# The experts' side work in another order: first weights of the next slot split a quarter sooner, the last conversion step inside the last quarter

## The chip, the core and the metric

The kernel runs on one core of one Trainium2 chip. The metric is device time in microseconds (us) of one execution; the time before is 1410.79 us, the median of three runs (1409.42 to 1414.0). The profiled execution is one more run of the same program, with a time of its own.

## The reference

Three layers follow each other. An attention without a product of queries and keys (the softmax of k over the tokens times v gives a 64 x 64 matrix for each head) makes 4608 tokens of 512 numbers. A mixture of eight experts sends every token to the expert with the largest gate logit:

```python
for e in range(E):
    mask = e_idx == e
    h = np.maximum(x[mask] @ w1[e], 0.0)
    out[mask] = gate_w[mask, None] * (h @ w2[e])
```

with w1[e] of 512 x 1024 and w2[e] of 1024 x 512. A dense layer `g = max(0.01 h, h)`, `h = x @ w_in`, `out = g @ w_out` (hidden width 2048) ends it; its weights arrive as 64-bit floats. All results are fp32.

## The kernel before, in words

**Products.** TensorE multiplies in a rounded 32-bit form. To keep fp32 accuracy, each operand is split into a high part (a cast on ScalarE, line 481) and a low part (source minus high part, a subtraction on VectorE, line 482), and each product is three matmuls: high by high, high by low, low by high. `split` is these two instructions.

**Slots.** The experts' tokens are worked off in slots of at most 512 tokens of one expert. Nine slots (0 to 8) always run; more run as the counts want, under a branch read from a register. In this input ten ran, the tenth (slot 9) in the half form with 256 rows.

A slot has two passes. The first, `pass1(f)` for f = 0 to 7, makes 128 hidden units each: 12 matmuls into a PSUM bank `hp`, then `hh` = relu (ScalarE, line 574) and `hl` = low part (VectorE, line 575). There are three `hp` banks, so the bank of f = 0 is wanted again by f = 3, and it is free once its `hl` is made. The second, `pass2(t)` for t = 0 to 3 (here called the four quarters), makes 128 output columns each: 24 matmuls into a bank `yp`, a copy `y` (ScalarE, line 589), and a store that ScalarE issues (line 590). After 12 of a quarter's 24 matmuls the function `mid` is called, and what it records stands on every engine in front of that quarter's copy.

**Side work.** While a slot is multiplied, the other engines do four things:
- `wsplit(s, which, c)` splits a quarter of a weight matrix: w2 of this slot in the first pass, w1 of the next slot (`w1h`, `w1l`) in the second. The source is a ring of six staging tiles `st`; each split lets SyncE issue the load of a later piece.
- `xload` at the slot's start turns token numbers into integers (`idi`, line 551) and gathers the next slot's rows into `xg`; `xgate` scales them; `xprep(k)` transposes them on TensorE (line 564, into `tp`, two PSUM banks) and splits them into `xh`, `xl`. `xprep(0)` and `xprep(1)` stand in the middle of quarter 1, `xprep(2)` and `xprep(3)` in the middle of quarter 2.
- `step()` runs one step of the conversion of the dense layer's weights from 64-bit floats: four steps make one conversion, and a slot has eight steps, two conversions. Step one also issues the two stores of the conversion before (`rh`, `rl`) and the loads for the next (`w`). Steps one to three are two VectorE instructions each. Step four is the heaviest: four sums `r` (line 631), a cast `rh` on ScalarE, and the subtraction `rl` on VectorE. It falls on f = 7 and on quarter 3.
- In slot 8 the step is a load of a weight of the dense layer, and `mid` of its quarter 3 also splits two operands of it.

**What sets the order.** Each engine runs its instructions in the order in which the Python code records them, and the framework adds the semaphores. No scheduler changes it here: where a call stands in `slot` is its place on each engine.

Of the kernel before, what the change touches and what calls it, by code (L numbers as in the profile page):

```python
# [25 lines left out]
NSLOT = 16  # L26
# [453 lines left out]
def split(nc, hi, lo, src):  # L480
    nc.scalar.copy(out=hi, in_=src)  # L481
    nc.vector.tensor_tensor(out=lo, in0=src, in1=hi.bitcast(F32), op=ALU.subtract)  # L482


def experts(ctx, tc, cst, a, region, xd, dense, did, wops, pre):
# [24 lines left out]
    def reg(s, f, mx):  # L510
        return nc.values_load(ti[0:1, 3 * s + f:3 * s + f + 1], engines=[SP] + [ACT] * (f == 2), min_val=0, max_val=mx)
# [17 lines left out]
    def loads_to(n):  # L529
        while nload[0] < min(n, len(items)):  # L530
            wload(*items[nload[0]])
            nload[0] += 1

    def wsplit(s, which, c):
        n = 8 * s + 4 * (which - 1) + c
        loads_to(n + 1)
        t = stage.pop((s, which, c))
        if which == 1:
            split(nc, w1h[:, :, 256 * c:256 * c + 256], w1l[:, :, 256 * c:256 * c + 256], t.rearrange("p (k f) -> p k f", k=4))
        else:  # L540
            split(nc, w2h[:, 2 * c:2 * c + 2], w2l[:, 2 * c:2 * c + 2], t.rearrange("p (k f) -> p k f", k=2))
        loads_to(n + 1 + AHEAD)

    def idload(s):
        if s < NSLOT:
            nc.sync.dma_start(out=idts[s % 3].rearrange("p t c -> p (t c)"),
                              in_=region[bass.ds(reg(s, 1, NE * NT), SLOT), :].rearrange("(p t) c -> p (t c)", t=4))

    def xload(s):
        idt, idi = idts[s % 3], idis[s % 2]  # L550
        nc.vector.tensor_copy(out=idi, in_=idt[:, :, 0])
        for t in range(4):
            nc.gpsimd.indirect_dma_start(out=xg[:, t], out_offset=None, in_=xd,  # L553
                                         in_offset=bass.IndirectOffsetOnAxis(ap=idi[:, t:t + 1], axis=0),
                                         bounds_check=NT - 1, oob_is_err=False)

    def xgate(s):
        for t in range(4):
            nc.scalar.activation(out=xg[:, t], in_=xg[:, t], func=AF.Copy, scale=idts[s % 3][:, t, 1:2])

    def xprep(k):
        tp = ps2.tile([128, 4, 128], F32, tag="tp", name="tp")
        for t in range(4):
            nc.tensor.transpose(out=tp[:, t], in_=xg[:, t, 128 * k:128 * k + 128], identity=ident)
        split(nc, *(x[:, k].rearrange("d (p t) -> d t p", t=4) for x in (xh, xl)), tp)

    def pass1(f, rows):
        hp = ps.tile([128, SLOT], F32, tag="h", name="hp")
        n = 0
        for k in range(4):  # L570
            for w, x in ((w1h, xh), (w1h, xl), (w1l, xh)):
                nc.tensor.matmul(hp[:, rows], lhsT=w[:, k, 128 * f:128 * f + 128], rhs=x[:, k, rows], start=(n == 0), stop=(n == 11))  # L572
                n += 1
        nc.scalar.activation(out=hh[:, f, rows], in_=hp[:, rows], func=AF.Relu)
        nc.vector.scalar_tensor_tensor(out=hl[:, f, rows], in0=hp[:, rows], scalar=0.0, in1=hh[:, f, rows].bitcast(F32),  # L575
                                       op0=ALU.max, op1=ALU.subtract)

    def pass2(d, o, mid, rows):
        yp = ps.tile([128, SLOT], F32, tag="y", name="yp")
        n = 0  # L580
        for f in range(8):
            for w, h in ((w2h, hh), (w2l, hh), (w2h, hl)):
                nc.tensor.matmul(yp[:, rows], lhsT=w[:, f, 128 * d:128 * d + 128], rhs=h[:, f, rows], start=(n == 0), stop=(n == 23))  # L583
                n += 1
            if f == 3:
                mid()
        y = ys[cnt[1] % 2]
        cnt[1] += 1
        nc.scalar.copy(out=y[:, rows], in_=yp[:, rows])
        nc.scalar.dma_start(out=dense[128 * d:128 * d + 128, bass.ds(o, rows.stop)], in_=y[:, rows])  # L590
# [65 lines left out]
    def slot(s, step=lambda: None, mid2=lambda t: None, rows=slice(0, SLOT)):  # L656
        if s + 1 < NSLOT:
            xload(s + 1)
        for f in range(8):
            pass1(f, rows)  # L660
            if f % 2 == 0:
                wsplit(s, 2, f // 2)
            else:
                step()
        if s + 1 < NSLOT:
            xgate(s + 1)
        o = reg(s, 2, NT)
        nc.sync.dma_start(out=did[bass.ds(o, SLOT)].rearrange("(p t) c -> p (t c)", t=4),
                          in_=idts[s % 3].rearrange("p t c -> p (t c)"))
        idload(s + 2)  # L670
        for t in range(4):
            def mid():
                if s + 1 < NSLOT and t in (1, 2):
                    xprep(2 * t - 2)
                    xprep(2 * t - 1)
                mid2(t)
            pass2(t, o, mid, rows)
            if s + 1 < NSLOT:
                wsplit(s + 1, 1, t)
            step()  # L680

    idload(0)
    loads_to(2)
# [9 lines left out]
    with ExitStack() as cctx:  # L693
        conv = conversions(cctx.enter_context(tc.tile_pool(name="cv", bufs=1, side="right", reuse_waits="tile")))
        next(conv)
        for s in range(NSTATIC - 1):
            slot(s, step=lambda: next(conv, None))
        for _ in conv:
            pass
    load, prep = pre()  # L700
    slot(NSTATIC - 1, step=lambda: next(load, None), mid2=lambda t: prep() if t == 3 else None)
    nb = nc.values_load(ti[0:1, 3 * NSLOT:3 * NSLOT + 1], min_val=0, max_val=NSLOT)
    ns = nc.values_load(ti[0:1, 3 * NSLOT + 1:3 * NSLOT + 2], min_val=NSTATIC, max_val=NSLOT)

    def more(s):
        if s == NSLOT:
            return
        with tc.If(ns > s):  # L708
            before = dict(stage), list(cnt), nload[0]
            regs.clear()  # L710
            with tc.If(nb > s) as big:
                slot(s)
            stage.clear()
            stage.update(before[0])
            cnt[:], nload[0] = before[1:]
            regs.clear()
            with big.Else():
                slot(s, rows=slice(0, SLOT // 2))
            regs.clear()
            more(s + 1)  # L720
# [393 lines left out]
```

## Time and profile before

| | |
|---|---|
| median of three runs | 1410.79 us |
| the profiled execution's own time | 1407.18 us |
| its span, first to last instruction | 1405.4 us |
| busy share TensorE / VectorE / ScalarE / GpSimd | 93% / 73% / 42% / 23% |
| mean granted TensorE clock | 0.974 |
| first matmul of slot 0, first matmul after slot 9 | 200.6 us, 657.45 us |

The experts are the stretch from 200.6 to about 657 us. To read them: the timeline of one engine gives each instruction's start and length, and in brackets how long the engine stood idle before it and what released it. A TensorE matmul is shown as longer than the distance to the next one, since matmuls overlap; the distance from start to start is what counts.

### The profile page before, as it was taken

The numbers are of one execution on the slowest core, as the hardware profiler recorded it, in microseconds if no ns is written. First come the engines' busy times: TensorE is split into PE (matmuls) and PEld (weight loads), VectorE is DVE, ScalarE is ACT, GpSimd is POOL, SyncE is SP. The second block draws the span as 40 slices with busy tenths as digits, with TensorE's granted clock in tenths as the row PEclk, the third lists the DMA queues.
The fourth block names the chain that finished last, engine by engine and source line by source line (L and its number), as shares of the span: only waits on it lengthen the run. The fifth ranks groups of instructions, "written<-read, shape, count | busy, mean of one in ns | idle before, by whom it ended". The sixth has DMA issues, their size and how long they took to land.

```text
span 1405.4 us, 23487 instructions
## 1 busy us (share of the span) xinstructions
PE 1306.8 (93%) x9179; PEld 1219.4 (87%) x9179; DVE 1029.1 (73%) x1392; ACT 585.5 (42%) x914; POOL 322.0 (23%) x279
## 2 busy tenths in 40 slices
PE   5989449999999999998999999999989999999998
PEld 5989337778777877788999999999989999999998
DVE  4788836776777677746777777787777777877785
ACT  3656235455545554555232333323233333333332
POOL 2225820110111011100333433434311111111111
PEclk9999769999999999998999999999999999999999
DMA  9773258787977797687933333233695443444330
GB/s 374 294 284 117 69 173 283 239 256 240 299 241 261 235 297 238 217 279 234 375 136 135 126 135 130 92 150 135 262 414 179 124 133 122 149 123 134 121 120 31
DMA packets 146969, 279.56 MB, mean 199 GB/s; under 512 B 18208, under 2 KB 70432, under 8 KB 145952
## 3 DMA queue, kind: packets, MB, share of 16 engines
q1 hardware_dynamic: 122064, 208.46, 44.0%
q10 hardware_dynamic: 17232, 48.48, 8.8%
q0 software_dynamic: 7552, 21.02, 4.2%
q8 instruction: 75, 1.23, 0.4%
q14 instruction: 46, 0.38, 0.1%
HBM read 181.59 MB, written 96.32 MB: 198 GB/s over the span
## 4 chain that ended last, share of the span: by engine, by line
issue 26%; DVE 8%; PE 8%; POOL 6%; DMA 3%; ACT 1%; POOLq 0%; SPq 0%; DVEq 0%; ACTq 0%
PE hp L801 8%; POOL out L982 3%; POOL s L841 2%; DMA wi<-wid 2%; DMA hd<-ht 2%; DVE ht L814 1%; DVE ht L847 1%; DVE ht L850 1%; DVE s L838 1%; DVE x L482 1%; DVE ht L834 1%; DVE s L836 1%; POOL s L842 1%; DVE xl L482 0%; ACT ht L843 0%
## 5 line engine op out<-in xcount | busy, mean ns | idle before, releaser
L801 PE MATMUL hp<-xh,wi 128*128 128x256 f32 x1152 | 212.9, 281 | 4.4 <-DVE ht L850 2.3
L960 PE MATMUL yp<-wi,x 128*128 128x256 f32 x1152 | 191.2, 283 | 0.3 <-DVE x L482 0.3
L801 PEld LDWEIGHTS hp<-xh,wi 128*128 128x128 f32 x1152 | 179.4, 188 | 7.0 <-DVE ht L850 3.5
L960 PE MATMUL yp<-wi,wi 128*128 128x256 f32 x1200 | 178.2, 283 | 0.3 <-DVE wi L482 0.3
L801 PE MATMUL hp<-x,wi 128*128 128x256 f32 x1296 | 164.2, 286 | 8.0 <-DVEq L708 6.5
L801 PEld LDWEIGHTS hp<-x,wi 128*128 128x128 f32 x1296 | 160.7, 194 | 8.3 <-ACTq L708 6.6
L960 PEld LDWEIGHTS yp<-wi,wi 128*128 128x128 f32 x1200 | 163.5, 192 | 0.5 <-DVE wi L482 0.5
L960 PEld LDWEIGHTS yp<-wi,x 128*128 128x128 f32 x1152 | 161.5, 192 | 0.6 <-DVE x L482 0.6
L801 PE MATMUL hp<-xl,wi 128*128 128x256 f32 x576 | 160.7, 279 | 0.0
L553 POOL DMA_INDIRECT xg<-xd,idi x44 | 55.4, 1259 | 399.4 <-DVE hl L575 349.6
L572 PE MATMUL hp<-xh,w1h 128*128 128x512 f32 (+1 forms) x320 | 122.9, 384 | 12.7 <-DVE hl L575 11.6
L583 PE MATMUL yp<-hh,w2h 128*128 128x512 f32 (+1 forms) x320 | 122.9, 384 | 0.0
L572 PE MATMUL hp<-xl,w1h 128*128 128x512 f32 (+1 forms) x320 | 121.5, 380 | 0.0
L583 PE MATMUL yp<-hl,w2h 128*128 128x512 f32 (+1 forms) x320 | 121.5, 380 | 0.0
L572 PE MATMUL hp<-xh,w1l 128*128 128x512 f32 (+1 forms) x320 | 121.4, 379 | 0.0
L583 PE MATMUL yp<-hh,w2l 128*128 128x512 f32 (+1 forms) x320 | 121.4, 379 | 0.0
L982 POOL DMA_INDIRECT out<-yo,idx x36 | 47.3, 1315 | 315.4 <-DVE idx L976 294.3
L482 DVE TENSOR_TENSOR w1l<-st,w1h 128x1024 fp32r<-128x1024 f32 x44 | 53.7, 1225 | 75.2 <-ACT w1h L481 75.1
L801 PEld LDWEIGHTS hp<-xl,wi 128*128 128x128 f32 x576 | 108.0, 187 | 0.0
L814 DVE SCALAR_TENSOR_TENSOR ht<-ht 128x1024 f32<-128x1024 f32 x72 | 104.9, 1457 | 2.5
L841 POOL TENSOR_TENSOR s<-s,s 128x512 f32<-128x512 f32 x36 | 48.6, 1351 | 207.9 <-DVE s L838 155.6
L843 ACT ACTIVATE ht<-s 128x512 f32<-128x512 f32 x36 | 22.8, 633 | 149.5 <-POOL s L842 145.1
(202 smaller groups left out, 2581.4 us busy)
## 6 DMA issues: line engine op xcount, KB each, us to landing
st<-in_w SPq DMA_DIRECT2D x89, 512.0 KB, 6.0
hd<-ht ACTq DMA_DIRECT2D x72, 512.0 KB, 3.0
xt<-hd SPq DMA_DIRECT2D x18, 1024.0 KB, 5.5
hr<-hd SPq DMA_DIRECT2D x18, 1024.0 KB, 5.5
wi<-wid SPq DMA_DIRECT2D x28, 512.0 KB, 10.7
wi<-wod SPq DMA_DIRECT2D x6, 2048.0 KB, 12.7
v<-in_v SPq DMA_DIRECT2D x16, 650.0 KB, 9.9
k<-in_k SPq DMA_DIRECT2D x16, 576.0 KB, 8.8
```

The lines of the kernel that those rows point to most:

```text
L482: nc.vector.tensor_tensor(out=lo, in0=src, in1=hi.bitcast(F32), op=ALU.subtract)
L553: nc.gpsimd.indirect_dma_start(out=xg[:, t], out_offset=None, in_=xd, in_offset=bass.IndirectOffsetOnAxis(ap=idi[:, t:t + 1], axis=0), bou ...
L572: nc.tensor.matmul(hp[:, rows], lhsT=w[:, k, 128 * f:128 * f + 128], rhs=x[:, k, rows], start=(n == 0), stop=(n == 11))
L583: nc.tensor.matmul(yp[:, rows], lhsT=w[:, f, 128 * d:128 * d + 128], rhs=h[:, f, rows], start=(n == 0), stop=(n == 23))
L801: self.nc.tensor.matmul(bank[:, g], lhsT=w[:, h, k, 128 * g:128 * g + 128], rhs=x[:, k], start=(n == 0), stop=(n == 5))
L814: V.scalar_tensor_tensor(out=c, in0=c, scalar=0.01, in1=c, op0=ALU.mult, op1=ALU.max)
L834: V.tensor_tensor(out=h[:, 0, 0], in0=bank, in1=s[1], op=ALU.add)
L836: V.tensor_tensor(out=s[6], in0=bank, in1=s[1], op=ALU.add)
L841: G.tensor_tensor(out=s[6], in0=s[6], in1=s[5], op=ALU.add)
L843: nc.scalar.activation(out=h[:, 1, 1], in_=s[5], func=AF.Relu)
L960: nc.tensor.matmul(bank, lhsT=x[:, k], rhs=w[i][:, h, k], start=(c == 0), stop=(c == 23))
L982: ins = nc.gpsimd.indirect_dma_start(out=out, out_offset=bass.IndirectOffsetOnAxis(ap=idi[s % 2][:, t:t + 1], axis=0), in_=y[:, t], in_off ...
```

## The change

In the second pass, the first quarter of the next slot's w1 is now split in the middle of quarter 0, and the other three at the ends of quarters 0, 1 and 2 (they stood at the ends of quarters 0 to 3). The conversion step of quarter 3, step four, moves from the end of that quarter to its middle, that is in front of the quarter's `y` copy. After quarter 3 nothing is left. No instruction is added or removed.

```diff
@@ -670,14 +670,20 @@
         idload(s + 2)
         for t in range(4):
             def mid():
-                if s + 1 < NSLOT and t in (1, 2):
-                    xprep(2 * t - 2)
-                    xprep(2 * t - 1)
+                if s + 1 < NSLOT:
+                    if t == 0:
+                        wsplit(s + 1, 1, 0)
+                    elif t < 3:
+                        xprep(2 * t - 2)
+                        xprep(2 * t - 1)
+                if t == 3:
+                    step()
                 mid2(t)
             pass2(t, o, mid, rows)
-            if s + 1 < NSLOT:
-                wsplit(s + 1, 1, t)
-            step()
+            if t < 3:
+                if s + 1 < NSLOT:
+                    wsplit(s + 1, 1, t + 1)
+                step()
```

The places shown are in slot 0; slots 1 to 7 have the same pattern with other staging tiles (`st_1999` to `st_2002` are the four pieces of w1 here).

On VectorE in quarters 0 and 1, from the subtraction `rl` of the conversion that ends in the first pass to the two `xl` of `xprep(0)` and `xprep(1)`:

```order
 L482 TENSOR_TENSOR rl<-r,rh 128x1792
 L482 TENSOR_TENSOR w1l<-st_1999,w1h 128x4x256
+L482 TENSOR_TENSOR w1l<-st_2000,w1h 128x4x256
 L618 TENSOR_SCALAR r<-w 128x1024
 L619 TENSOR_SCALAR r<-r 128x1024
 L482 TENSOR_TENSOR xl<-tp,xh 128x4x128 x2
-L482 TENSOR_TENSOR w1l<-st_2000,w1h 128x4x256
+L482 TENSOR_TENSOR w1l<-st_2001,w1h 128x4x256
```

The second piece now stands in front of the conversion step and of the two `xl`.

On ScalarE at the same place, before:

```order
L589 COPY y_2009<-yp 128x512
L590 REGISTER_ALU
L590 DMA dense<-y_2009 128x512
L481 CAST w1h<-st_1999 128x4x256
L481 CAST xh<-tp 128x4x128 x2
```

and after the change:

```order
L481 CAST w1h<-st_1999 128x4x256
L589 COPY y_2009<-yp 128x512
L590 REGISTER_ALU
L590 DMA dense<-y_2009 128x512
L481 CAST w1h<-st_2000 128x4x256
L481 CAST xh<-tp 128x4x128 x2
```

One cast more stands in front of the pair of `xh`.

On VectorE from quarter 2 to the end of the slot:

```order
 L482 TENSOR_TENSOR xl<-tp,xh 128x4x128 x2
-L482 TENSOR_TENSOR w1l<-st_2001,w1h 128x4x256
+L482 TENSOR_TENSOR w1l<-st_2002,w1h 128x4x256
 L626 TENSOR_TENSOR r<-r,w 128x1024
 L627 SCALAR_TENSOR_TENSOR r<-w,r 128x1024
-L482 TENSOR_TENSOR w1l<-st_2002,w1h 128x4x256
 L631 TENSOR_TENSOR r<-r 128x256 x4
 L482 TENSOR_TENSOR rl<-r,rh 128x1792
```

The fourth piece no longer stands between step three (lines 626, 627) and step four (line 631 and `rl`).

On ScalarE from the end of quarter 2 to the next slot's first relu, before:

```order
L481 CAST w1h<-st_2001 128x4x256
L589 COPY y_2010<-yp 128x512
L590 ISA
L590 DMA dense<-y_2010 128x512
L481 CAST w1h<-st_2002 128x4x256
L481 CAST rh<-r 128x1792
L574 ACTIVATE hh<-hp 128x512
```

and after the change:

```order
L481 CAST w1h<-st_2002 128x4x256
L481 CAST rh<-r 128x1792
L589 COPY y_2010<-yp 128x512
L590 ISA
L590 DMA dense<-y_2010 128x512
L574 ACTIVATE hh<-hp 128x512
```

The cast `rh` now has quarter 3's copy and store behind it.

On SyncE, which issues the loads and the conversions' stores, at the end of quarter 0:

```order
 L523 DMA st_1998<-in_w 128x2x512
+L523 ISA
+L523 DMA st_1999<-in_w 128x2x512
 L635 DMA wid_64<-rh 896x1x256
 L636 DMA wid_64<-rl 896x1x256
 L602 DMA w<-in_win 128x2x512 x2
```

The load into `st_1999`, which waits until that tile has been split, now stands in front of the two stores and of the loads for the next conversion.

## Rows read from the trace of the kernel before

**Rows 1.** The page's head and its line of TensorE: busy us (share) xinstructions.
```profile
span 1405.4 us, 23487 instructions
PE 1306.8 (93%) x9179; PEld 1219.4 (87%) x9179; DVE 1029.1 (73%) x1392; ACT 585.5 (42%) x914; POOL 322.0 (23%) x279
```

**Rows 2.** Waits: who waited for whom, us in total, times, longest us.
```profile
PE hp L572 <- DVE hl L575: 11.6, 9, 2.3
```

**Rows 3.** Timeline of TensorE, slot 2's start; last row slot 8: start us, us, operation, [idle<-releaser].
```profile
296.55 0.39 PE L572 MATMUL hp<-xh,w1h 128*128 128x512 f32 x1
...
304.48 0.39 PE L572 MATMUL hp<-xh,w1l 128*128 128x512 f32 x1
306.04 0.50 PE L572 MATMUL hp<-xh,w1h 128*128 128x512 f32 x1 [1.17 <-DVE hl L575]
306.37 0.39 PE L572 MATMUL hp<-xl,w1h 128*128 128x512 f32 x1
...
587.12 0.50 PE L572 MATMUL hp<-xh,w1h 128*128 128x512 f32 x1 [1.17 <-DVE hl L575]
```

**Rows 4.** One period by windows: us, busy of PE PEld DVE ACT POOL, clock, DMA.
```profile
296.55:343.40 46.85, 45.68 (x210) 37.62 (x209) 35.43 (x44) 24.50 (x30) 5.12 (x4) 1.00 0.82 259
```

**Rows 5.** Timeline of VectorE, from slot 1's last quarter into slot 2.
```profile
293.39 1.23 DVE L482 TENSOR_TENSOR w1l<-st,w1h 128x1024 fp32r<-128x1024 f32 x1 [1.99 <-ACT w1h L481]
294.53 1.22 DVE L626 TENSOR_TENSOR r<-r,w 128x1024 int32<-128x1024 int32 x1
295.79 1.22 DVE L627 SCALAR_TENSOR_TENSOR r<-w,r 128x1024 int32<-128x1024 int32 x1
...
299.97 1.55 DVE L631 TENSOR_TENSOR r<-r 128x256 f32<-128x256 f32 x4
303.28 2.02 DVE L482 TENSOR_TENSOR rl<-r,rh 128x1792 fp32r<-128x1792 f32 x1 [1.76 <-ACT rh L481]
...
305.30 0.68 DVE L575 SCALAR_TENSOR_TENSOR hl<-hp,hh 128x512 fp32r<-128x512 f32 x1
```

**Rows 6.** Timeline of ScalarE, the same place.
```profile
301.56 1.70 ACT L481 CAST rh<-r 128x1792 fp32r<-128x1792 f32 x1 [2.76 <-DVE r L631]
303.16 0.58 ACT L574 ACTIVATE hh<-hp 128x512 fp32r<-128x512 f32 x1
```

**Rows 7.** Timeline of ScalarE, VectorE and TensorE, slot 1's quarters 0 to 2.
```profile
280.06 0.57 ACT L589 COPY y<-yp 128x512 f32<-128x512 f32 x1
...
281.05 1.05 ACT L481 CAST w1h<-st 128x1024 fp32r<-128x1024 f32 x1 [0.42 <-ACT y L589]
282.00 2.01 ACT L481 CAST xh<-tp 128x512 fp32r<-128x512 f32 x2
...
282.13 1.22 DVE L482 TENSOR_TENSOR w1l<-st,w1h 128x1024 fp32r<-128x1024 f32 x1 [2.37 <-ACT w1h L481]
...
284.60 2.05 DVE L482 TENSOR_TENSOR xl<-tp,xh 128x512 fp32r<-128x512 f32 x2
...
287.47 1.03 PE L564 MATMUL tp<-cf,xg 128*128 128x128 f32 x8
```

**Rows 8.** Timeline of VectorE, TensorE and SyncE's queue, slot 9's second pass and end.
```profile
643.85 2.12 DVE L482 TENSOR_TENSOR xl<-tp,xh 128x512 fp32r<-128x512 f32 x2
...
645.42 1.26 PE L564 MATMUL tp<-cf,xg 128*128 128x128 f32 x8
...
651.33 0.37 SPq L523 DMA_DIRECT2D st<-in_w  x1
...
657.45 7.21 PE L801 MATMUL hp<-x,wi 128*128 128x256 f32 x36 [6.45 <-DVEq L708]
```

**Rows 9.** By tile, 636 to 660 us: issue to landing of `st`, then of `dense`.
```profile
DMA to landing us min/median/max: 3.9/4.4/5.8
...
DMA to landing us min/median/max: 2.4/3.5/4.3
```

**Rows 10.** By tile, the whole span: issue to landing of the stores of `rh`.
```profile
DMA to landing us min/median/max: 4.1/4.4/4.7
```

## The prediction

> **What bounds the kernel now.** I read the page first, then TensorE's waits, then the timeline of each engine around the wait that repeats. The page gives TensorE 93% of the span [rows 1], so what TensorE stands idle for in the stretch that is edited is what can be won. The waits name one thing there: nine times a matmul of the first pass waited for `hl`, 11.6 us in all, the longest 2.3 us [rows 2]. The longest is in slot 0, before any edited place; the other eight are (11.6 - 2.3) / 8 = 1.16 us each, one in every slot from 1 to 8. Two of them are in the rows, at 306.04 and 587.12; they lie six slots apart, so a slot takes 281.08 / 6 = 46.85 us [rows 3]. In one such period TensorE is busy 45.68 of 46.85 us, and the clock is granted in full (1.00, that is 2.4 GHz); VectorE is busy 35.43 us and ScalarE 24.50 us [rows 4]. So TensorE sets the pace of a slot but for one bubble, and the other engines have the time for their work: only its order is late.
>
> The bubble costs more than its 1.17 us of idle time. Slot 2's first 36 matmuls start from 296.55 to 304.48, 35 distances of 0.2266 us [rows 3]. At that pace the next two would start at 304.71 and 304.93; they start at 306.04 and 306.37. The second is 1.44 us late, and that is what a slot loses.
>
> Why the bank is late: it belongs to f = 0, and VectorE makes its `hl` only at 305.30, for 0.68 us, right after `rl` (303.28, 2.02 us) [rows 5]. `rl` waits for the cast `rh` on ScalarE (301.56), that waits for the four sums `r` (299.97), and these stand behind the fourth w1 piece, which waits for quarter 3's copy. ScalarE's relu of f = 0 stands behind the same cast, at 303.16 [rows 6]. So the slot's first two results wait for the heaviest conversion step.
>
> **The change, part by part.**
>
> *Quarter 3.* The fourth w1 piece takes the place that the third had: 293.39 on VectorE. Step three follows as before, 294.53 and 295.79, and ends at 297.01. Now nothing stands between it and the four sums: they start at 297.0 instead of 299.97, 2.97 us sooner [rows 5]. From there the distances are those of before: the cast 1.59 us later (298.6), `rl` 1.72 us after that (300.3), `hl` 2.02 us after that (302.3 to 303.0). On ScalarE the `y` copy of quarter 3 now stands behind the cast: it starts 1.60 us after it (303.16 less 301.56 [rows 6]) at 300.2, and with its store takes 0.99 us of the queue (281.05 less 280.06 [rows 7]), so the relu of f = 0 starts at 301.2 and ends at 301.8, still before VectorE wants it. The bank is free at 303.0, and TensorE asks for it at 304.71: a margin of 1.7 us. What is late next is f = 1: its `hl` follows one w2 piece (1.2 us) and ends at about 304.9, wanted one group of 12 matmuls later, at 307.4. After that VectorE waits for TensorE, as it does now from f = 3 on. So I take the whole bubble as gone in each of the eight slots: 8 x 1.44 = 11.5 us. The bounds are 0 (it stays) and 11.5 us (more than all of it can't go). The copy that now comes some 3.5 us later holds a `yp` bank; there are three, and this one is wanted again two quarters into the next second pass, so TensorE covers that.
>
> *Quarters 0 to 2.* The first piece's cast takes the copy's place at 280.06; the copy follows 0.95 us later, the second cast 0.99 us after that at 282.00, and the two `xh` at 282.95 instead of 282.00 [rows 7]. VectorE follows: it starts a `w1l` 1.08 us after its cast (282.13 less 281.05), so the second piece goes at 283.08 where the first had gone at 282.13, and all behind it is 0.95 us later. The two `xl` end at 287.60 instead of 286.65. Who waits for them: TensorE's transposes of `xprep(2)` and `xprep(3)` at 287.47, which reuse the two `tp` banks. The first bank is free at 286.6, in time. The second is wanted by the fifth transpose, some 0.44 us into the eight, at 287.91; it is free at 287.66 (a wait is over 0.06 us after the end of what it waited for: 305.98 against 306.04). The margin is a quarter of a microsecond. I take 0. The other end is a wait as long as the shift itself plus what a restart costs over its idle time, 0.95 + 0.27 = 1.2 us in eight slots, 9.8 us lost.
>
> *SyncE.* The load into the first piece's tile now waits for a split that ends at 282.4 and stands in front of the stores of `rh` and `rl` and of the next conversion's loads; they go out some 4.5 us later than now. `rh` is overwritten by the cast at 298.6, 16 us after that, and its store lands 4.1 to 4.7 us from issue [rows 10]; the conversion that needs the loads starts in the next slot, over 20 us on. I cost this at nothing: the distance to the next use hides it.
>
> *The end of slot 9.* It has half the rows, so a quarter lasts half as long while the side work stays. The two `xl` at 643.85 (1.06 us each) become 644.80, and end at 645.9 and 646.9; TensorE wants the banks at 645.42 and about 645.9 [rows 8]. Here the 0.95 us does become a wait, about 1.0 us. Against it: TensorE then stands 6.45 us until 657.45, since the branch's end waits for every transfer in flight, and the last weight load goes out only at 651.33 [rows 8] and takes up to 5.8 us [rows 9], that is to 657.1. It waits for the third piece's split, which comes a quarter sooner. The last to land is then the store of quarter 3 (the load goes before it if it is out by 650.2): TensorE ends at 652.0 instead of 651.0, copy and issue end at 652.5, and with the median landing of 3.5 us [rows 9] it is there at 656.0, 1.1 us sooner than 657.1. I take 1.0 us gained; with landings of 2.4 and of 5.8 us the ends are 2.1 us gained and 1.2 us lost.
>
> **Sum.** The profiled execution took 1407.18 us, 1.8 us more than its span [rows 1]. Less 11.5 and 1.0 us that is 1394.7 us. The median of the runs shown, 1410.79 us, lies 3.6 us above the profiled one, so on their scale I forecast 1410.8 - 12.5 = 1398.3 us.
>
> **A rule that speaks against it.** The row shows the same bubble in eight slots, on a PSUM bank. The Trainium skill (Perfetto Trace Analysis, Optimization Strategy) says that a gap repeating on the engine that should be saturated can mean there is too little SBUF or PSUM for the next tile. By that, three `hp` banks would be too few, and an order that adds none would leave the gap: 1409.8 us, the second rival. The trace speaks for the order: the bank is late behind a conversion step that doesn't use it, and the same three banks cause no wait later in the pass.
>
> **The rivals.**
> - *The transposes take over.* The quarter microsecond is within what I can read off: ScalarE stands 0.42 us idle before a cast that follows a store [rows 7], and one more such pause gives a wait of 0.2 us, 0.5 us with its restart. In eight slots that is 4 us back: 1402.3 us. At the other end above (9.8 us) it is 1408 us. For it: nothing else has so thin a margin. Against: by the rows it just holds.
> - *The bubble is one of banks and stays,* or moves to f = 1: only the 1.0 us at the end is won, 1409.8 us. Against it stands the margin of 1.7 us, and 2.5 us at f = 1.
> - *Slower: the cast at the head of ScalarE's queue.* From 293.4 on ScalarE has `rh` at its head, with quarter 3's copy and the relu of f = 0 behind it. If the store of the last `rh`, issued at 282.4 and now behind one load more, hasn't landed, all three wait, then `rl` and `hl`. It decides against the change when the cast starts after 301.56, when it starts now: a landing over 19 us after issue. Each microsecond more costs eight: at 20.2 us it is 1410.8 - 1.0 + 8 = 1417.8 us. Against it: a landing of 4.7 us at most, and one more weight load in front, at 5.8 us [rows 9], makes 10.5.
>
> **Chances.** The forecast 0.81, the transposes 0.10, the bubble that stays 0.05, the slower one 0.04. About 0.3%, 4.2 us, is what a measurement of this kernel can tell from no change. The first case and nearly all of the second are faster by more than that: 0.90. The third and the rest of the second are within it: 0.06. The last is slower: 0.04. The forecast's own ends are -12.5 with 1 us either way from slot 9, and about 2 us for which run is the median. Upward the range takes in the transposes' likelier half, to 1405: 1394 to 1405.
>
> **What would show it.** Right: TensorE's waits for `hl` fall from nine to one, slot 0's, and the distance from slot to slot falls from 46.85 to 45.4 us. The first `hl` of a slot starts about 2.4 us before its bank is wanted. The first matmul after slot 9 comes at about 645 us. Wrong: waits of line 564 for `xl` in slots 0 to 7; or waits for `hl` that remain; or ScalarE's `rh` waiting for a transfer. A wait of line 564 in slot 9, about 1 us, is expected.

## The result and the profile after

The changed kernel takes 1400.01 us, the median of five runs (1399.2 to 1402.99), against 1413.76 us for the kernel before beside it (1409.42 to 1415.85): a ratio of 0.9908, with a 95% interval of 0.9895 to 0.9922. That is 13.8 us faster; 12.5 us were forecast.

The profiled execution after has an own time of 1399.21 us. Its page, as [rows 1]:

```profile
span 1397.4 us, 23488 instructions
PE 1303.5 (93%) x9179; PEld 1219.2 (87%) x9179; DVE 1030.4 (74%) x1392; ACT 585.3 (42%) x914; POOL 320.4 (23%) x279
```

TensorE's busy time fell by 3.3 us (1306.8 before); the rest of what went is idle time. Its waits from 195 to 660 us after, against [rows 2] (lines behind 690 stand six further down: L801 of before is L807 now, L708 is L714):

```profile
PE hp L807 <- PEq L714: 2.7, 1, 2.7
PE hp L572 <- DVE hl L575: 2.1, 1, 2.1
PE tp L564 <- DVE xl L482: 1.7, 2, 1.4
PE hp L572 <- ACT y L589: 0.8, 1, 0.8
```

Nine waits for `hl` are one, slot 0's. Of the two for `xl`, 1.4 us lie ahead of slot 0 and 0.35 us in slot 9; the one for `y`, 0.84 us, stands in front of slot 9's first matmul, as before (1.10). Within slots 1 to 8 TensorE waits for nothing. TensorE's timeline where slot 2 and slot 3 begin, and the window between:

```profile
300.08 0.39 PE L572 MATMUL hp<-xh,w1h 128*128 128x512 f32 x1
...
308.25 0.39 PE L572 MATMUL hp<-xh,w1h 128*128 128x512 f32 x1
...
345.46 0.39 PE L572 MATMUL hp<-xh,w1h 128*128 128x512 f32 x1
```

```profile
300.10:345.50 45.40, 45.40 (x210) 37.73 (x209) 35.59 (x44) 24.50 (x30) 4.83 (x4) 1.00 0.85 265
```

A slot takes 345.46 - 300.08 = 45.38 us (46.85 before; slots 1 to 7 all 45.37 or 45.38), and TensorE is busy in all of it; VectorE and ScalarE do the same work as in [rows 4]. At 308.25 the slot asks for its first bank again (36 matmuls after its first). VectorE's timeline before that, as [rows 5], then ScalarE's, as [rows 6]:

```profile
296.93 1.23 DVE L482 TENSOR_TENSOR w1l<-st,w1h 128x1024 fp32r<-128x1024 f32 x1 [1.53 <-ACT w1h L481]
298.07 1.22 DVE L626 TENSOR_TENSOR r<-r,w 128x1024 int32<-128x1024 int32 x1
299.32 1.23 DVE L627 SCALAR_TENSOR_TENSOR r<-w,r 128x1024 int32<-128x1024 int32 x1
300.58 1.55 DVE L631 TENSOR_TENSOR r<-r 128x256 f32<-128x256 f32 x4
303.90 2.03 DVE L482 TENSOR_TENSOR rl<-r,rh 128x1792 fp32r<-128x1792 f32 x1 [1.76 <-ACT rh L481]
...
305.91 0.68 DVE L575 SCALAR_TENSOR_TENSOR hl<-hp,hh 128x512 fp32r<-128x512 f32 x1
...
302.17 1.70 ACT L481 CAST rh<-r 128x1792 fp32r<-128x1792 f32 x1 [5.28 <-DVE r L631]
303.77 0.58 ACT L589 COPY y<-yp 128x512 f32<-128x512 f32 x1
...
304.76 0.60 ACT L574 ACTIVATE hh<-hp 128x512 fp32r<-128x512 f32 x1 [0.42 <-ACT y L589]
```

The four sums now start right behind line 627, and the chain cast, `rl`, `hl` follows at the old distances. The bank is free at 306.59, 1.66 us before it is wanted; 1.7 us were forecast. The cast waited for `r` and for no store.

The end of slot 9, as [rows 8]: TensorE's transposes, SyncE's last weight load, ScalarE's issue of the last store, TensorE's restart.

```profile
639.42 0.66 PE L564 MATMUL tp<-cf,xg 128*128 128x128 f32 x4 [0.35 <-DVE xl L482]
...
641.00 0.37 SPq L523 DMA_DIRECT2D st<-in_w  x1
...
644.84 0.34 ACTq L590 DMA_DIRECT2D dense<-y  x1
...
647.10 3.10 PE L807 MATMUL hp<-x,wi 128*128 128x256 f32 x24 [2.70 <-PEq L714]
```

The last load goes out 3.8 us before the last store now; before, both went out together (651.33 and 651.43), and TensorE stood 6.45 us. It stands 2.70 us now.

**Where the time went.** From slot 0's first matmul to the first after slot 9 it was 456.81 us and is 647.10 - 205.42 = 441.68: 15.1 us less, 11.8 up to slot 9's first matmul (seven slots by 1.47, slot 8 by 1.7, of which 0.26 is the shorter wait for `y` at its end, slot 0 0.2 longer) and 3.3 in slot 9 and its end. The dense stage gives 2.3 us back: from the restart to the span's end 747.95 us before, 750.30 after. And this execution came to slot 0 4.8 us later than that of before (205.42 against 200.64), in code that the change doesn't touch. The spans differ by -15.1 + 2.3 + 4.8 = -8.0 us; a second execution of the changed kernel (below) starts slot 0 at 200.48.

### The profile page after: what moved, and what is told of

Read it like the earlier page. It is cut to its first block, busy times and chain, and to the rows that moved or that the text cites. A ratio compares the mean times of both kernels' runs of the same rounds, so it can differ in the third digit from the quotient of the medians.

```text
span 1397.4 us, 23488 instructions
## 1 busy us (share of the span) xinstructions
PE 1303.5 (93%) x9179; PEld 1219.2 (87%) x9179; DVE 1030.4 (74%) x1392; ACT 585.3 (42%) x914; POOL 320.4 (23%) x279
## 4 chain that ended last, share of the span: by engine, by line
issue 27%; DVE 10%; POOL 7%; PE 5%; DMA 3%; ACT 1%; POOLq 0%; SPq 0%; DVEq 0%
PE hp L807 5%; POOL out L988 3%; POOL s L847 2%; DMA wi<-wid 2%; DVE ht L820 2%; DVE ht L853 1%; DMA hd<-ht 1%; DVE ht L856 1%; DVE s L844 1%; DVE ht L840 1%; DVE s L842 1%; DVE x L482 1%; POOL s L848 1%; DVE xl L482 0%; ACT ht L849 0%
## 5 line engine op out<-in xcount | busy, mean ns | idle before, releaser
L807 PE MATMUL hp<-xh,wi 128*128 128x256 f32 x1152 | 212.8, 281 | 3.8 <-DVE ht L856 2.4
L807 PEld LDWEIGHTS hp<-xh,wi 128*128 128x128 f32 x1152 | 179.4, 188 | 6.5 <-DVE ht L856 3.9
L807 PE MATMUL hp<-x,wi 128*128 128x256 f32 x1296 | 163.3, 285 | 7.4 <-DMA wi<-wid 4.0
L807 PEld LDWEIGHTS hp<-x,wi 128*128 128x128 f32 x1296 | 159.6, 193 | 8.0 <-DVE ht L820 4.2
L807 PE MATMUL hp<-xl,wi 128*128 128x256 f32 x576 | 160.7, 279 | 0.0
L807 PEld LDWEIGHTS hp<-xl,wi 128*128 128x128 f32 x576 | 108.0, 187 | 0.0
L847 POOL TENSOR_TENSOR s<-s,s 128x512 f32<-128x512 f32 x36 | 48.6, 1350 | 211.2 <-DVE s L844 158.9
L574 ACT ACTIVATE hh<-hp 128x512 fp32r<-128x512 f32 (+1 forms) x80 | 46.2, 577 | 98.1 <-PE hp L572 94.3
```

Of the source, the lines that this page charges most:

```text
L807: self.nc.tensor.matmul(bank[:, g], lhsT=w[:, h, k, 128 * g:128 * g + 128], rhs=x[:, k], start=(n == 0), stop=(n == 5))
L847: G.tensor_tensor(out=s[6], in0=s[6], in1=s[5], op=ALU.add)
```

## The experiments

All times are medians beside runs of the kernel before on the same chip; ratios are to those, with 95% intervals. "Experts" is the stretch from slot 0's first matmul to the first after slot 9, "gap" TensorE's idle time at its end, "dense" from there to the span's end, each from the one profiled execution.

| kernel | median us | ratio | experts us | gap us | dense us |
|---|---|---|---|---|---|
| before (first profile) | 1413.76 beside the changed kernel, then 1409.26, 1408.19, 1409.29 | 1 | 456.81 | 6.45 | 747.95 |
| changed (first profile) | 1400.01 | 0.9908 [0.9895, 0.9922] | 441.68 | 2.70 | 750.30 |
| split_only | 1397.35 | 0.9908 [0.9894, 0.9922] | 443.65 | 2.51 | 750.10 |
| step_only | 1399.85 | 0.9931 [0.9917, 0.9945] | 446.97 | 6.71 | 752.96 |
| last_only | 1407.28 | 0.9984 [0.9973, 0.9996] | 453.48 | 2.44 | 751.43 |
| static_only | 1400.48 | 0.9941 [0.9927, 0.9955] | 444.42 | 6.54 | 752.09 |
| before_banks | 1395.99 | 0.9906 [0.9889, 0.9923] | 444.84 | 6.77 | 748.92 |
| after_banks | 1394.91 | 0.9902 [0.9887, 0.9918] | 440.72 | 2.24 | 750.38 |
| push_two | 1402.02 | 0.9950 [0.9931, 0.9968] | 449.59 | 2.16 | 750.21 |
| after_again | 1394.28 | 0.9896 [0.9879, 0.9913] | 441.28 | 2.79 | 750.04 |
| after_late | 1391.03 | 0.9858 [0.9843, 0.9874] | 442.10 | 3.00 | 745.68 |
| before_late | 1404.70 | 0.9971 [0.9959, 0.9983] | 458.97 | 6.59 | 745.70 |

**split_only: the splits alone.** Step four stays behind quarter 3.

The edit against the changed kernel:

```diff
-                if t == 3:
-                    step()
                 mid2(t)
...
-            if t < 3:
-                if s + 1 < NSLOT:
-                    wsplit(s + 1, 1, t + 1)
-                step()
+            if t < 3 and s + 1 < NSLOT:
+                wsplit(s + 1, 1, t + 1)
+            step()
```

> Only the splits move (first piece in the middle of quarter 0, the others at the ends of quarters 0 to 2); the conversion step stays at the end of quarter 3. Theory (order): the bank of f = 0 was late because the heavy step stood behind the fourth piece, which waits for quarter 3's copy; without that piece the four sums start right after step three all the same. So all eight waits for hl go, from the first matmul of slot 0 to the first after slot 9 it is about 442 us as with the whole change (457 before), and the ratio to before is about 0.991. Rival (the step must also be ahead of the copy): the waits stay at 0.5 us or more, and the ratio lies above 0.994.

Its waits of TensorE from 205 to 660 us (line 804 is here what 801 was before):

```profile
PE hp L572 <- DVE hl L575: 3.0, 1, 3.0
PE hp L804 <- DVEq L711: 2.5, 1, 2.5
PE hp L572 <- ACT y L589: 1.0, 1, 1.0
...
PE tp L564 <- DVE xl L482: 0.3, 1, 0.3
```

Only slot 0's wait for `hl` is left, and the gap is short. The move of the splits does all that the whole change does: slots 1 to 7 take 45.37 us here too. (Its experts' stretch is 2 us longer by slot 0 alone, which takes 48.6 to 51.4 us over these executions, 49.29 in the changed kernel's and 51.35 in this one.)

**step_only: the conversion step alone.** The splits stay at the ends of quarters 0 to 3. Against the kernel before:

```diff
+                if t == 3:
+                    step()
                 mid2(t)
...
-            step()
+            if t < 3:
+                step()
```

> Only the conversion step of quarter 3 moves to its middle; the splits stay at the quarters' ends, the fourth one after quarter 3. Theory (order): the step now stands before the fourth piece, the four sums start some 3 us sooner, and the fourth piece follows the subtraction rl; hl of f = 0 starts about 1.2 us later than with the whole change and still about 1.2 us before its bank is wanted. All eight waits go; slot 9 ends as before (idle 6.45 us, clock falling). About 445 us for the experts, ratio about 0.992. Rival (the fourth piece in front of hl costs it the margin): waits of 0.3 us or more remain in slots 1 to 8, ratio above 0.994.

```profile
PE hp L804 <- DVEq L711: 6.7, 1, 6.7
PE hp L572 <- DVE hl L575: 3.1, 1, 3.1
PE hp L572 <- ACT y L589: 1.1, 1, 1.1
```

The eight bubbles are gone here too: step four comes out from behind the last w1 piece either way. But the last piece is still split behind quarter 3, its load goes out late, and the gap stays. So of the two parts of the change each cures the bubbles alone, and only the move of the splits shortens the gap.

**last_only and static_only: one stretch alone.** The changed order in the slots under the branch only (the first diff, against the kernel before), and in slots 0 to 8 only (the second).

```diff
+                    if t == 0:
+                        if s >= NSTATIC:
+                            wsplit(s + 1, 1, 0)
...
-            if s + 1 < NSLOT:
+            if s < NSTATIC:
                 wsplit(s + 1, 1, t)
-            step()
+                step()
+            elif t < 3 and s + 1 < NSLOT:
+                wsplit(s + 1, 1, t + 1)
```

```diff
+                    if t == 0:
+                        if s < NSTATIC:
+                            wsplit(s + 1, 1, 0)
...
+                if t == 3:
+                    step()
...
-            if s + 1 < NSLOT:
-                wsplit(s + 1, 1, t)
-            step()
+            if s >= NSTATIC:
+                if s + 1 < NSLOT:
+                    wsplit(s + 1, 1, t)
+            elif t < 3:
+                wsplit(s + 1, 1, t + 1)
+                step()
```

> The changed order only in the slots under the branch (here slot 9), the old order in slots 0 to 8. Theory (the branch's end waits for the last transfer): the eight waits of 1.17 us stay; the idle time of TensorE after slot 9 falls from 6.45 to about 2.7 us and the clock doesn't fall there; the dense stage then waits for its first weights and gives most of that back, so the total is about 1 us less, ratio 0.999. Rival (the gap at the branch's end belongs to the branch itself): idle 6 us as before, ratio 1.000.

> The changed order in slots 0 to 8, the old one in the slots under the branch. Theory: the eight waits are gone, 11.5 us; slot 9 ends with about 6.4 us of idle time and the clock at half as before; ratio about 0.992, 1 us behind the whole change. Rival (the gain at the end of slot 9 comes from the earlier slots' work being done sooner): idle about 2.7 us there too, and the same time as the whole change, 0.991.

In last_only the waits of before stand beside a short gap:

```profile
PE hp L572 <- DVE hl L575: 12.1, 9, 2.8
PE hp L807 <- DVEq L714: 2.4, 1, 2.4
```

The two are independent: static_only shortens the experts by 12.4 us and keeps the gap, last_only shortens them by 3.3 us. But last_only's 3.3 us end as 2.0 us in its time (1409.26 - 1407.28), and its dense stage is 3.5 us longer than that of before. static_only's is 4.1 us longer too and step_only's 5.0; in these two SyncE's first load for it follows TensorE's restart by 2.07 and 3.25 us (0.87 before). static_only's ratio, 0.9941, misses the 0.992 that was expected.

**before_banks and after_banks: one PSUM bank more.** Four banks for `hp`, two for `yp`, in the old and in the new order.

```diff
-    np_ = ps.tile([128, NE], F32, tag="h", name="np")
+    np_ = ps.tile([128, NE], F32, tag="h", name="np", bufs=4)
...
-        hp = ps.tile([128, SLOT], F32, tag="h", name="hp")
+        hp = ps.tile([128, SLOT], F32, tag="h", name="hp", bufs=4)
...
-        yp = ps.tile([128, SLOT], F32, tag="y", name="yp")
+        yp = ps.tile([128, SLOT], F32, tag="y", name="yp", bufs=2)
```

> The order of the kernel before; only the PSUM banks differ: four for hp instead of three, two for yp instead of three. Theory of the order: the slot's first hl is late (305.98 in slot 2) because of the conversion step in front of it, and any 2.7 us more of slack at that place cures it. With four banks the first one is wanted by f = 4, at about 307.4, so the eight waits for hl go and slot 0's 2.1 us too; the gap after slot 9 stays at 6.4 to 6.7 us, and the dense stage gives about 1 us back. Ratio to the kernel before 0.990 to 0.993. By the rule of the bubble that is one of banks it is the same ratio, and the two theories agree here: the run tells what more slack is worth beside the order. Rival: two yp banks are too few, a matmul of the second pass waits for the copy y; some 0.5 us in each of four quarters of eight slots, 16 us, and the ratio is 1.00 or above.

> The changed order with four banks for hp and two for yp. If the order has already cured all that the banks could, only slot 0's wait for hl (2.1 us, 2.3 with its restart) is left to win: ratio 0.989 to 0.990, some 2 us under the changed kernel run beside it. If the changed order still lost something to the banks in slots 1 to 8 that the waits don't show, the gain is 4 us or more: 0.987. Rival: quarter 3's copy, which now stands behind the cast rh, holds one of only two yp banks, and the second pass waits for y: 0.992 or above.

All of before_banks' waits of TensorE on lines 564 and 572, from 205 to 660 us:

```profile
PE tp L564 <- ACT xg L559: 0.6, 2, 0.3
PE hp L572 <- issue: 1.2, 1, 1.2
```

(On `issue` it waits for nothing that the profile shows; this one stands in front of slot 9.) No wait for `hl` is left, slot 0's neither, with the old order: ratio 0.9906, as the change. So the bubble was a want of 1.2 us of slack, and a bank buys it as well as the order. What the bank doesn't buy is the gap (6.77 us). In the new order the bank has almost nothing left to do: slot 0's 1.7 us go, but TensorE comes to slot 0's transposes sooner and waits there five times (three times 0.28 us for `xg`, then 0.22 and 0.34 us for `xl`). Slot 0 takes 48.92 us, 48.58 in after_again, and the experts are 0.6 us shorter than there, at their end, not the 2 us that were expected. The two ratios overlap: no order or bank tried beats the changed kernel by what can be measured.

**push_two: the thin margin, overdrawn.** From the changed kernel, the third piece is split at the end of quarter 0 beside the second.

```diff
-                if s + 1 < NSLOT:
+                if s + 1 < NSLOT and t != 1:
                     wsplit(s + 1, 1, t + 1)
+                    if t == 0:
+                        wsplit(s + 1, 1, 2)
```

> The changed order, but the third piece of w1 is split at the end of quarter 0, beside the second, so that a second split stands in front of the two xl of quarter 1, and none at the end of quarter 1. If the margin at the transposes in the middle of quarter 2 is as thin as forecast (a quarter of a microsecond with two tp banks), the xl come about 1.0 us later again and TensorE waits for them on line 564 in each of slots 0 to 8: 0.7 to 0.8 us of wait each, with the restart about 1 us in nine slots, 8 to 9 us back, ratio 0.996 to 0.998. If the margin is wider than 1 us, no wait of line 564 in slots 0 to 8 and a ratio of 0.991 as the changed kernel.

Its TensorE around the transposes in the middle of slot 1's quarter 2, and VectorE's `xl` of quarter 1:

```profile
286.32 2.06 DVE L482 TENSOR_TENSOR xl<-tp,xh 128x512 fp32r<-128x512 f32 x2
...
286.92 0.39 PE L583 MATMUL yp<-hl,w2h 128*128 128x512 f32 x1
287.45 0.66 PE L564 MATMUL tp<-cf,xg 128*128 128x128 f32 x4
288.44 0.66 PE L564 MATMUL tp<-cf,xg 128*128 128x128 f32 x4 [0.33 <-DVE xl L482]
288.85 0.48 PE L583 MATMUL yp<-hh,w2h 128*128 128x512 f32 x1
```

And the same place in the changed kernel:

```profile
289.04 2.08 DVE L482 TENSOR_TENSOR xl<-tp,xh 128x512 fp32r<-128x512 f32 x2
...
290.77 0.39 PE L583 MATMUL yp<-hl,w2h 128*128 128x512 f32 x1
291.00 1.03 PE L564 MATMUL tp<-cf,xg 128*128 128x128 f32 x8
291.79 0.48 PE L583 MATMUL yp<-hh,w2h 128*128 128x512 f32 x1
```

In the changed kernel the second `xl` ends at 291.12 and its bank is wanted 0.44 us into the eight, at 291.44: 0.32 us, or 0.26 with the 0.06 us that the forecast took off for the release (forecast 0.25). In push_two the `xl` ends at 288.38, and the eight fall in two: from the matmul before them to the one behind 1.93 us instead of 1.02, of which the listed wait shows only 0.33. That is 0.91 us a slot: slots 1 to 7 take 46.24 to 46.30 us, and the experts are 8.3 us longer than in after_again (6.4 in these seven; slot 8, which has no conversion step, loses nothing, slot 0 is 1.7 longer). The cost was as expected; the listed wait was less than half of the one expected, and the ratio ends just under the expected stretch. The margin was real and as thin as read.

**after_again: the changed kernel once more.**

> The changed kernel once more, beside the three others. Ratio 0.990 to 0.992. In its profile the experts' stretch (first matmul of slot 0 to the first after slot 9) is again 441 to 443 us, and the gap after slot 9 2.4 to 2.8 us. The attention stage's start of slot 0 (205.4 us in the first profile, 200.6 before) tells whether those 4.8 us belong to the change or to the execution: in 200.5 to 203 if to the execution, at 205 again if to the change.

The experts' stretch is 441.28 us, 15.5 less than before, and slot 0 begins at 200.48: the 4.8 us belong to the first execution. The spans now differ by 1391.8 - 1405.4 = -13.6 us, -15.5 from the experts, +2.1 from the dense stage and -0.2 ahead of slot 0. At the gap this execution shows a landing that the first trace lacks; issue to landing of the `y` stores in the last 6.8 us before the restart:

```profile
DMA to landing us min/median/max: 1.9/3.1/4.4
```

The 1.9 us are the last store's: issued at 639.41, 3.8 us behind the last weight load (which landed at 639.66), restart at 641.76. In step_only, with a load issued 0.1 us ahead of it, the least is 3.1 us, the last store's again:

```profile
DMA to landing us min/median/max: 3.1/3.5/3.9
```

The other traces that show the last store's landing agree: 1.8 to 2.1 us where the load went out 3.8 us ahead or more, 3.0 to 3.3 us where it went out 0.1 us ahead. A load in flight is not enough for the longer one: after_again's store at 629.18, 2.85 us behind a load that landed only at 630.56, landed in 1.80 us.

But the landings are not what lets TensorE go. Before, the load issued at 651.33 lands in 4.6 us, at 655.89, and TensorE starts 1.56 us after that, released by VectorE's sequencer ([rows 8]; the load's landing):

```profile
DMA to landing us min/median/max: 4.6/4.6/4.6
```

In after_banks the last store, issued at 638.92, lands at 640.74, when TensorE has started (in push_two too: 650.22, start 650.19):

```profile
DMA to landing us min/median/max: 1.8/1.8/1.8
...
640.72 6.20 PE L807 MATMUL hp<-x,wi 128*128 128x256 f32 x36 [2.24 <-DVEq L714]
```

In both executions of the change the releaser is TensorE's own sequencer (`PEq`). Of its two branch instructions at the branch's end the longer takes 4.4 us, in the first execution from 642.10 to 646.53 (ns, min/median/max):

```profile
L714 PEldq COMPARE_BRANCH  x2: 192/2310/4428, 642.1 to 646.7; - x2
```

What the twelve profiles do show: where the last load goes out behind quarter 3, five of them, the gap is 6.45 to 6.77 us; where it goes out sooner, seven, 2.16 to 3.00. From its branch instruction to its next one ScalarE takes 5.2 to 5.5 us in the five and 2.4 to 2.6 in the seven, VectorE 4.3 to 4.6 and 2.8 to 3.2. Why is open. In the five the fourth piece's cast and subtraction stand behind quarter 3 as well (VectorE ends them at 654.17 before), and no run tells the load from the split.

**after_late and before_late: is the dense stage bound by its loads?** In nine of the ten profiles so far TensorE waits for a weight `wi`, 33 to 37 us after its restart. After (TensorE, SyncE's first loads), then before:

```profile
682.22 2.09 PE L807 MATMUL hp<-x,wi 128*128 128x256 f32 x11 [3.98 <-DMA wi<-wid]
...
647.77 3.44 SPq L777 DMA_DIRECT2D wi<-wid  x7
```

```profile
691.77 1.42 PE L801 MATMUL hp<-x,wi 128*128 128x256 f32 x10 [1.50 <-DMA wi<-wid]
...
658.32 3.48 SPq L771 DMA_DIRECT2D wi<-wid  x7
```

It ends 34.45 us after SyncE's first load in the one, 33.45 in the other. So these two kernels let seven loads, the awaited one among them, go out a unit later; the fourth unit multiplies by the weights of the third instead and leaves out its own, so that nobody reads them early:

```diff
-                if u in (0, 1):
-                    self.wload(u + 2, i)
+                if u in (0, 2):
+                    self.wload(3 if u else 2, i)
...
-                self.product(q, i, bank)
+                self.product(2 if u == 3 else q, i, bank)
```

> The changed kernel; in the dense stage the seven loads of the hidden weights of quarter q = 3 go out in the third unit instead of the second, and the fourth unit (the first that would read them) multiplies by the weights of q = 2 instead. That leaves out that unit's own weights and nothing else; no load is saved, seven of them only have no reader for some 40 us more. Theory (the dense stage's start is bound by the loads from the moment SyncE leaves the branch, so that the sooner restart after slot 9 is given back there): the wait for wi, 3.7 to 4.1 us some 35 us after the restart, is gone, and from the restart to the span's end it takes about 746 us instead of 750.0 to 750.4. Time about 4 us under the changed kernel: ratio to the kernel before about 0.987. Rival (the 2 us more in the dense stage come from its end or from the clock): the restart to the end stays at 749 us or more although the wait is gone.

> The kernel before with the same edit of the dense stage, and the same left out. Theory: its wait for wi was only 1.8 to 2.0 us, since TensorE comes back later than SyncE's loads begin and runs the first 5 us at the low clock; so only about 2 us are won, the restart to the end is about 746 us, as in the changed kernel with this edit, and the two differ by about 15.5 us in time, 2 us more than without the edit: ratio 0.998 to 0.999. Rival: both gain the same, the difference stays at 13.5 to 14 us.

All of after_late's waits of TensorE over 1 us from 640 us on:

```profile
PE yp L966 <- issue: 5.7, 1, 5.7
PE hp L807 <- PEq L714: 3.0, 1, 3.0
PE hp L807 <- DVE ht L856: 2.3, 6, 0.4
PE hp L807 <- ACT s L834: 1.5, 6, 0.3
```

The wait for `wi` is gone in both, and the dense stage takes 745.68 and 745.70 us, 4.4 to 4.6 and 2.3 us less than with it: equal now. So what was given back hangs on this wait, by one profile of each kernel. Not all of it lies there: the wait ends 34.3 us after the restart before, 35.1 in the first execution of the change and 35.8 in after_again, which is 0.8 and 1.5 us later. Most of the rest of the first one's 2.3 us is another gap, at line 966 (960 before), of 6.5 us for 5.0; over the twelve profiles it is 4.9 to 6.5 us, and differs between executions of one kernel. The times don't settle it by themselves: the medians lie 13.7 us apart where 15.5 were expected, and that is what the rival (both gain the same) foretold; the ratio of the two ratios, 0.9858 / 0.9971 = 0.9887, would be 15.9 us, and the intervals hold both.

## Why the prediction was right, point by point

*The bubbles.* Right in mechanism and size: 11.5 us forecast, 7 x 1.47 + 1.7 = 12.0 us measured in slots 1 to 8, of which 0.26 us is the shorter wait in front of slot 9. The chain started as soon as foreseen, and the bank's margin was 1.66 us for 1.7.

*Quarters 0 to 2.* Right: margin 0.26 for 0.25 us, no wait in slots 0 to 8. push_two shows what stood behind it: 0.91 us a slot once one split more stands in front of the `xl`.

*SyncE.* Right: the stores of `rh` and `rl` went out 3.6 and 2.1 us later in the slot (4.5 were forecast), and nobody waited for them.

*The end of slot 9.* Right in direction, wrong in mechanism and size: 1.0 us was taken, 3.3 us measured, beyond even the better end of 2.1. The wait at the transposes was taken as 1.0 us; the two `xl` came only 0.44 us later there, not 0.95 (18.55 us after slot 9's first matmul for 18.11), and TensorE works from slot 9's first matmul to its last in 25.70 us instead of 25.26, so it cost 0.44. The step that failed is the other: that the branch's end waits for every transfer in flight, so that the last landing sets TensorE's restart. It made the last load land at 657.1, by the longest of its row (5.8 us, [rows 9]); that load landed at 655.89, 1.56 us before the restart, and in after_banks and push_two TensorE starts before the last store has landed. The store's own landing was taken at 3.5 us and took 1.9 in after_again, less than the least in its row (2.4). What did hold is that the gap shortens when the last load goes out sooner: 6.45 to 2.70 us. What ends it stays open.

*What the sum lacked.* It stopped at the restart after slot 9. Behind it TensorE waits for a load of the dense stage, and the stage as a whole was 2.1 to 2.3 us longer. SyncE's loads do start as much sooner as TensorE (0.67 and 0.70 us after its restart, 0.87 before). But TensorE is ready for the awaited one 31.1 and 31.7 us after its restart, 32.8 before, and the wait ends 34.45 and 35.10 us after SyncE's first load, 33.45 before; why these loads take longer is open. So 11.8 + 3.3 - 2.3 = 12.8 us stand against 12.5: two errors nearly cancel, 2.3 too little at the exit and 2.3 given back unseen. That the total came so close is luck, as far as these two go; the 11.8 us are not. The timed medians differ by 13.8 us; the ratio's interval, 11.0 to 14.8 us, holds both.

*The rivals.* The transposes took over in slot 9 alone. The slower case did not come: the cast `rh` waited for `r`. The rule of repeating gaps in the Trainium skill (Perfetto Trace Analysis, Optimization Strategy) had a right remedy and would have given a wrong time: one more bank does cure the bubbles (before_banks, 0.9906), but so does an order that adds none (0.9908).

*What would show it.* The waits fell from nine to one and the period to 45.4 us, as told, and a slot's first `hl` starts 2.34 us before its bank is wanted (2.4 forecast). The restart at about 645 us came at 647.10, that is 642.3 if slot 0's later start is taken off, and 641.76 in after_again.

## What to carry to other kernels

Where the same wait repeats on a PSUM bank, ask which instruction stood in front of the one that frees it: splits moved, a step moved or one bank more each took the same 1.47 us off slots 1 to 7 here, and a second cure on top gave nothing. Don't end a sum at the last edited place: follow the gain into the next stage, here to a wait for its loads. And before a landing is made the end of a gap, check in the trace that the engine starts after it, and who releases it.

## What the runs showed of the hardware

A short gap doesn't always keep TensorE's clock. After gaps of 6.45 to 6.77 us the first 5 us were granted 0.50 to 0.68 in all five profiles that have one (0.50 is 1.2 GHz throughout). After gaps of 2.16 to 3.00 us it was 1.00 in four (push_two 2.16, last_only 2.44, split_only 2.51, changed 2.70) but 0.66 in after_banks (2.24) and in after_again (2.79), and 0.50 in after_late (3.00). Two executions of the changed kernel, by windows of 5 us from the restart, the first, then after_again:

```profile
647.10:652.10 5.00, 4.26 (x33) 4.06 (x34) 4.29 (x7) 2.83 (x6) 0.00 (x0) 1.00 0.68 214
```

```profile
641.76:646.76 5.00, 5.00 (x29) 5.00 (x30) 4.26 (x7) 2.81 (x6) 0.00 (x0) 0.66 0.69 231
```

In the length of the dense stage it doesn't show: 750.30 and 750.04 us. But the first has 1.6 us more in its gap at line 966 (6.5 for 4.9), so a cost of a microsecond or so isn't excluded. What makes the clock fall in one execution and not in the other is open.
